# Twelve empty VectorE instructions ahead of the last two copies of a decode kernel

## The chip, the cores and the metric

One core of a Trainium2 chip (trn2). The metric is the device time of one execution in microseconds (us). A few executions of each kernel are compared on one chip.

## The reference, cut to what matters

One token goes through a pre-norm decoder block: attention over a cache of 32 heads x 4096 positions x 128, a residual, a layer norm, and a gated MLP with tanh GELU.

```python
x = A_x
h = x + _A_ref(_layernorm(x), A_k_cache, A_v_cache, A_wq, A_wo)
h2 = h + _B_ref(_layernorm(h), B_w_gate, B_w_up, B_w_down)   # GLU of 1728, down to 640
```

## The kernel before

The kernel records each operation with what it depends on, per engine, and emits waits and signals from that. Only its end matters here: the GLU product `hm`, the down projection, the copies and the store.

```python
ga = glu(ps_g, wg_sb, range(5), hl, d_wg)          # TensorE, 75 matmuls
glu(ps_u, wu_sb, range(3), d_wu[0])                # TensorE, 45
up = glu(ps_u, wu_sb, range(3, 5), d_wu[1])        # TensorE, 30
# ... GELU of the gate on VectorE and ScalarE, g1 to g8 ...
g6 = V(lambda e: e.tensor_mul(gu[:, :], g_t[:, :], t1[:, :]), g8)
g9 = V(lambda e: e.tensor_mul(hm[:, :], gu[:, :], ps_u[:, 0:15]), g6, up)
# ... down() : matmuls of hm with the down weights, 4 quarters of the result ...
T(down([13, 14]), g9, d_wp)
T(down(range(4)), d_wd[0])
T(down(range(4, 8)), d_wd[1])
T(down(range(8, 12)), d_wd[2])
dn = {q: T(down([12], [q]), d_wd[3]) for q in (0, 2, 1, 3)}
os = [V(lambda e, q=q: e.tensor_copy(out_row[0:1, 160 * q:160 * q + 160], ps_d[32 * q:32 * q + 1, 0:160]), dn[q])
      for q in range(2)]
os += [A(lambda e, q=q: e.copy(out_row[0:1, 160 * q:160 * q + 160], ps_d[32 * q:32 * q + 1, 0:160]), dn[q])
       for q in range(2, 4)]
d_out = P.dma("sync", out[0, :, :], out_row[:, :], *os)
```

`V`, `A`, `T` and `P.op` record an operation for VectorE, ScalarE, TensorE or a named engine; what follows the function are its dependencies.

The softmax here doesn't subtract the row's maximum and nothing guards it: scores larger than these inputs give would overflow.

Of the kernel before, what the change touches and what calls it, by code (L numbers as in the profile page):

```python
# [180 lines left out]
def bass_sequential_preLN__gqa_block_cached__glu_gated_geglu__decode_kernel(nc, A_x, A_k_cache, A_v_cache, A_wq, A_wo, B_x, B_w_gate, B_w_up, B_w_down, out):  # L181
# [60 lines left out]
    P = Prog(nc)  # L242
# [265 lines left out]
    g6 = V(lambda e: e.tensor_mul(gu[:, :], g_t[:, :], t1[:, :]), g8)  # L508
    g9 = V(lambda e: e.tensor_mul(hm[:, :], gu[:, :], ps_u[:, 0:15]), g6, up)

    def down(ms, qs=range(4)):
        def fn(e):
            for m in ms:
                for q in qs:
                    rows, wd = (128, wd_sb[:, m]) if m < 13 else (48, wd_lo[:, m - 13])
                    i = e.matmul(ps_d[32 * q:32 * q + 1, 0:160], hm[0:rows, m:m + 1],  # L516
                                 wd[0:rows, 160 * q:160 * q + 160], start=False, stop=(m == 12))
            return i
        return fn
# [5 lines that stand above are left out]
# [36 lines left out]
```

## Time and profile before

| | before |
|---|---|
| device time, 3 runs | 202.89 us median (202.81 to 203.33) |
| span of the profile | 201.4 us |
| last down weights landed | 198.64 us |
| VectorE idle between `hm` and its first copy | 3.12 us |
| TensorE idle for the last load | 0.61 us |

The first two rows are the whole, the last three are the place of the change. Here the loads set the end (transfers are 85% of the chain that ended last), so the engines have slack; the question is how much of it lies just where the change adds work. The profile lines for this are in the prediction.

### The profile page before, as it was taken

The page shows a single profiled execution, that of the slowest core. Times are in us where ns is not written, and L with a number is a line of the kernel's source. Part 1 is how long each engine was busy: PE and PEld are TensorE (multiplying, and loading weights), DVE is VectorE, ACT ScalarE, POOL GpSimd, SP SyncE. Part 2 cuts the span into 40 slices and gives each one's busy share as a digit, 9 for nine tenths or more (in the row PEclk, how much of TensorE's full clock was granted, in tenths as well). Part 3 has the DMA queues.
Part 4 walks back from the last instruction along what each step waited for, and adds up shares of the span by engine and source line. Part 5 has one row for each costly group of instructions (what it writes and reads, how often), then busy time and mean ns, then how long its engine had stood idle before and what let it go on. Part 6 is the DMA issues. An engine that isn't in the chain of part 4 may idle for free.

```text
span 201.4 us, 2003 instructions
## 1 busy us (share of the span) xinstructions
PE 119.7 (59%) x1009; PEld 33.8 (17%) x756; DVE 100.9 (50%) x51; ACT 12.6 (6%) x33; POOL 34.4 (17%) x36
## 2 busy tenths in 40 slices
PE   0107009659617943696299257907791697678684
PEld 0101000001200020112010201200201012268572
DVE  0200098983598079605970994199209933220321
ACT  2100000001000100010001001000000010010101
POOL 6400000000090018000900350053004400100000
PEclk9999757978966985589769859995599589685555
DMA  9989999999999999999999999999999999999992
GB/s 325 439 387 462 442 429 423 416 423 459 442 429 423 423 423 429 456 436 436 416 423 423 442 442 436 436 423 416 429 449 436 436 429 403 431 419 423 412 410 98
DMA packets 3848, 84.30 MB, mean 419 GB/s; under 512 B 450, under 2 KB 644, under 8 KB 1156
## 3 DMA queue, kind: packets, MB, share of 16 engines
q1 hardware_dynamic: 3842, 84.23, 97.8%
q8 instruction: 4, 0.07, 0.1%
q10 hardware_dynamic: 2, 0.00, 0.0%
HBM read 84.23 MB, written 0.00 MB: 418 GB/s over the span
## 4 chain that ended last, share of the span: by engine, by line
DMA 85%; PE 10%; SPq 4%; issue 0%; DVE 0%
DMA v_slot<-in_A_v_cache_dram 71%; DMA k_slot<-in_B_w_down_dram 13%; PE psum L363 9%; SPq L59 4%; PE psum L516 0%; DVE out_row L525 0%
## 5 line engine op out<-in xcount | busy, mean ns | idle before, releaser
L375 DVE TENSOR_TENSOR prod<-k_slot,qb 128x8192 bf16<-128x8192 bf16 x16 | 75.2, 4736 | 6.1 <-DMA k_slot<-in_A_k_cache_dram 6.1
L167 PE MATMUL psum<-prod,id_b 128*128 128x512 bf16 x233 | 65.0, 434 | 0.0
L381 DVE TENSOR_REDUCE sc<-psum 128x128 f32<-128x2048 f32 x8 | 18.3, 2291 | 50.7 <-PE psum L167 50.7
L385 POOL TENSOR_TENSOR p_bd<-pt,own 128x512 bf16<-128x512 bf16 x6 | 28.3, 4716 | 87.2 <-ACT pt L382 87.2
L352 PE MATMUL psum<-prod,id_b 128*128 128x512 bf16 x23 | 10.4, 452 | 49.4 <-DVE prod L375 46.2
L363 PE MATMUL psum<-v_slot,p_bd 128*16 128x512 bf16 x224 | 18.3, 484 | 7.4 <-DMA v_slot<-in_A_v_cache_dram 7.4
L352 PEld LDWEIGHTS psum<-prod,id_b 128*128 128x128 bf16 x23 | 2.3, 99 | 69.6 <-DVE prod L375 52.2
L369 PEld LDWEIGHTS psum<-hs,po_sb 128*128 128x128 f32 x64 | 8.3, 191 | 24.1 <-issue 23.5
L363 PEld LDWEIGHTS psum<-v_slot,p_bd 128*16 128x16 bf16 x224 | 5.8, 105 | 38.9 <-DMA v_slot<-in_A_v_cache_dram 30.7
L392 ACT COPY po_sb<-psum 128x512 f32<-128x512 f32 x7 | 4.1, 586 | 73.3 <-PE psum L363 73.3
L369 PE MATMUL psum<-hs,po_sb 128*128 128x4 f32 x64 | 7.7, 244 | 0.4 <-ACT po_sb L428 0.4
L382 ACT ACTIVATE pt<-sc,zero_t 128x128 bf16<-128x128 f32 x8 | 3.2, 401 | 70.4 <-DVE sc L381 70.4
L335 PE MATMUL psum<-arena,xlnB 128*32 128x512 bf16 x20 | 3.1, 579 | 7.3 <-DMA arena<-in_A_wq_dram 7.3
L465 PE MATMUL psum<-aP,arena 128*128 128x1 bf16 x160 | 6.7, 178 | 0.7 <-DMA arena<-in_A_wo_dram 0.6
L465 PEld LDWEIGHTS psum<-aP,arena 128*128 128x128 bf16 x160 | 6.6, 131 | 0.9 <-DMA arena<-in_A_wo_dram 0.7
L389 POOL MEMSET spare<- 1x1 f32 x1 | 0.1, 89 | 35.6 <-DVE p_bd L385 35.6
L494 PE MATMUL psum<-hlnT,v_slot 128*128 128x1 bf16 x150 | 5.5, 173 | 0.7 <-issue 0.7
L340 DVE CAST qb<-psum 128x512 bf16<-128x512 f32 x1 | 0.7, 692 | 9.8 <-PE psum L167 9.8
L494 PEld LDWEIGHTS psum<-hlnT,v_slot 128*128 128x128 bf16 x150 | 5.4, 120 | 1.3 <-issue 0.7
L363 PE MATMUL psum<-k_slot,p_bd 128*16 128x512 bf16 x32 | 3.5, 616 | 2.8 <-DVE p_bd L385 2.8
L308 PE MATMUL psum<-one_bf,x_row 1*128 1x1 bf16 x5 | 0.4, 177 | 7.1 <-DMA x_row<-in_A_x_dram 7.1
L311 DVE COPY xx<-psum 128x5 f32<-128x5 f32 x1 | 0.2, 165 | 7.5 <-PE psum L308 7.5
(73 smaller groups left out, 34.2 us busy)
## 6 DMA issues: line engine op xcount, KB each, us to landing
k_slot<-in_A_k_cache_dram SPq DMA_DIRECT2D x8, 4096.0 KB, 26.3
v_slot<-in_A_v_cache_dram SPq DMA_DIRECT2D x7, 4096.0 KB, 17.0
arena<-in_A_wq_dram SPq DMA_DIRECT2D x1, 5120.0 KB, 15.6
arena<-in_A_wo_dram SPq DMA_DIRECT2D x2, 2560.0 KB, 33.7
k_slot<-in_A_v_cache_dram SPq DMA_DIRECT2D x1, 4096.0 KB, 25.2
v_slot<-in_B_w_gate_dram SPq DMA_DIRECT2D x1, 2160.0 KB, 24.7
k_slot<-in_B_w_down_dram SPq DMA_DIRECT2D x3, 640.0 KB, 30.1
v_slot<-in_B_w_up_dram SPq DMA_DIRECT2D x1, 1296.0 KB, 27.4
```

What stands on the lines that cost most here:

```text
L59: ev = self.op(eng, lambda e: e.dma_start(out, in_), *deps, dma=True, chan=chan)
L167: built = e.matmul(out, lhsT, rhs, start=start, stop=stop)
L352: mm = held if n or not first else lambda e, *a, **k: e.matmul(*a, **k)
L363: i = e.matmul(ps_o[a:a + 16, :], p_bd[:, 4 * b:4 * b + 4, :].rearrange("p g j -> p (g j)"), vt[:, 4 * b:4 * b + 4, :], start=(b < 4), sto ...
L369: i = e.matmul(ps_a[:, bass.ds(at, 4)], po_sb[:, 128 * r:128 * r + 128], hs[:, r, :], start=(r == 0), stop=(r == 3))
L375: mults[G, i] = VM(lambda e: e.tensor_tensor(out=prod[:, i, :, :], in0=kt[:, 64 * i:64 * i + 64, :], in1=qb[:, G, :].unsqueeze(1).to_broad ...
L381: reds[G] = VR(lambda e: e.reduce_sum(sc[:, :], ps_f.rearrange("p (g d) -> p g d", d=16), axis=AX.X), folds[G, 1])
L382: exps[G] = AS(lambda e: e.activation(pt[:, :], sc[:, :], ACTF.Exp, bias=zero_t[:, 0:1], scale=INV_SQRT_DH, accum_out=RS[:, G:G + 1]), red ...
L385: blocks[G] = on(lambda e: e.tensor_tensor(out=p_bd[:, :, :], in0=pt[:, :].unsqueeze(2).to_broadcast([128, 128, 4]), in1=own[:, :].unsquee ...
L392: evs[G] = AS(lambda e: e.copy(po_sb[:, :], ps_o), pvs[G])
L465: r = e.matmul(ps_p[:, c:c + 1], wo_sb[:, i, c::5], aP[:, i:i + 1], start=False, stop=(i == 31), skip_group_check=True)
L494: i = e.matmul(ps[:, m:m + 1], ws, hlnT[:, c:c + 1], start=(c == 0 and m == 0), stop=(c == 4), skip_group_check=True)
```

## The change

The intent is to see what instructions that do nothing cost in VectorE's stream, at a place where VectorE has to wait. Each carries the flag `nofuse`.

```diff
     g9 = V(lambda e: e.tensor_mul(hm[:, :], gu[:, :], ps_u[:, 0:15]), g6, up)
 
+    def idle(eng, n):
+
+        def fn(e):
+            for _ in range(n):
+                i = e.nop(hint="n", nofuse=True)
+            return i
+        return P.op(eng, fn)
+    idle("vector", 12)
+
     def down(ms, qs=range(4)):
```

## The prediction

> **What bounds the kernel now.** I read the chain that ended last first, because an addition can cost only where it lengthens that chain, and took its shares from the page and its last pieces from the chain in order of time, cut to 163 to 201.5 us.
>
> ```profile
> span 201.4 us, 2003 instructions
> ...
> DMA 85%; PE 10%; SPq 4%; issue 0%; DVE 0%
> ```
>
> ```profile
> 171.63 27.02 DMA k_slot<-in_B_w_down_dram
> 198.64 0.04 issue
> 198.69 0.88 PE psum L516 x18
> 199.56 0.30 DVE out_row L525
> 199.86 0.03 issue
> 199.89 0.32 DVE out_row L525
> ```
>
> The transfers are 85% of the chain. The whole kernel is a stream of loads at a mean of 419 GB/s, and the last piece of the down weights lands at 198.64 us. What follows it is short and serial: the last down matmuls (0.88 us), two copies of the result on VectorE (0.30 and 0.32 us), then the store. VectorE is 50% busy over the span, but that average says nothing of this change: it adds VectorE work at one place only, so I read that place. It lies after the GLU product (L509, `hm`) and before the copies (L525). The timeline of VectorE alone, 196 to 201.4 us:
>
> ```profile
> 196.26 0.17 DVE L509 TENSOR_TENSOR hm<-gu,psum 128x15 bf16<-128x15 f32 x1 [1.86 <-PE psum L494]
> 199.55 0.66 DVE L525 CAST out_row<-psum 1x160 bf16<-1x160 f32 x2 [3.12 <-PE psum L516]
> ```
>
> The bracket is the number that decides the case: VectorE has nothing to do for 3.12 us (196.26 + 0.17 = 196.43 to 199.55), and what ends the idle time is TensorE's L516. What does TensorE do in that gap? The timeline of all engines, same stretch:
>
> ```profile
> 196.49 0.43 PE L516 MATMUL psum<-wd_lo,hm 48*1 48x160 bf16 x8 [0.33 <-DVE hm L509]
> ...
> 196.85 1.23 PE L516 MATMUL psum<-k_slot,hm 128*1 128x160 bf16 x32
> ...
> 198.69 0.83 PE L516 MATMUL psum<-k_slot,hm 128*1 128x160 bf16 x20 [0.61 <-DMA k_slot<-in_B_w_down_dram]
> ...
> 199.59 0.60 ACT L527 CAST out_row<-psum 1x160 bf16<-1x160 f32 x2 [5.89 <-PE psum L516]
> ```
>
> TensorE runs the down projection in three groups, and before the third it idles 0.61 us for the load that lands at 198.64 us. So the 3.12 us are held open at their far end by a DMA and 0.88 us of matmuls, neither of which asks VectorE for anything after `hm`. The other two quarters of the result are copied by ScalarE at 199.59 us and end at about the same time (199.59 + 0.60 = 200.19 against VectorE's 199.55 + 0.66 = 200.21).
>
> [...] No nop is in the trace of before[...]; its nearest relative there is the bare wait instruction on VectorE's sequencer:
>
> ```profile
> L114 DVEq EVENT_SEMAPHORE  x5: 21/21/116, 20.5 to 196.2; - x5
> ```
>
> Its columns are minimum, median and maximum in ns: 21 ns in the usual case. [...]
>
> **The change, part by part.** Removed: nothing. Moved: nothing; no load, buffer, semaphore or dependency changes. Added: 12 nops in VectorE's stream, which wait for nothing and signal nothing; they carry a flag[...], so I take all twelve to be there.
>
> Cost of the twelve, in three sizes, all estimates from numbers above:
> - Low: 12 x 21 ns = 0.25 us.
> - What I believe: [...]the pitch some two to three times the reported 21 ns, 40 to 65 ns, so 12 x 50 ns = 0.6 us. The factor is my choice; nothing in the trace gives it.
> - High: a nop that goes through VectorE's pipeline like a small dependent instruction. The timeline has such a row at 192.76, 192.97 and 193.18 us (L501, L502, L503, 128x15 each), a pitch of 0.21 us. 12 x 0.21 = 2.52 us.
>
> Where they lie: the first can start [...]when it has ended, 196.43 us. They are done by 196.43 + 0.6 = 197.03 us in the middle case and by 196.43 + 2.52 = 198.95 us in the high one. The first copy cannot start before 199.55 us. So 2.5 us of the gap stay unused in the middle case and 0.6 us in the high one. On the path: 0. `hm` stands before the nops in the same stream and signals when it ends, so TensorE gets it no later than now. Sum: 202.89 + 0 = 202.89 us.
>
> **The rivals.**
> 1. *The nops are dear.* The gap is used up at 3.12 / 12 = 260 ns each; beyond that every ns counts twelve times, as VectorE's copies end last. To reach 2% (0.02 x 202.89 = 4.06 us) each would have to take (3.12 + 4.06) / 12 = 598 ns. At 400 ns the time would be 202.89 + 4.8 - 3.12 = 204.6 us, still under 1% more. Against it: the 21 ns of a sequencer instruction, and that even a pass through the pipeline is 0.21 us.
> 2. *Code fetch.* Twelve more instructions could push VectorE's program over a block boundary and start a fetch late, among saturated queues. For it: the page shows fetches inside the span.
>
> ```profile
> q8 instruction: 4, 0.07, 0.1%
> ```
>
> Against it: [...]VectorE has 51 counted instructions[...]. And a fetch would come in a gap of 3 us. [...]
> 3. *`hm` is delayed.* If the twelve ran ahead of L509 or held its signal, the first two down groups would come later by 0.6 us, but TensorE idles 0.61 us for the last load anyway, so the time would stay at 202.9 us. For the high cost of 2.52 us it would be 202.89 + 2.52 - 0.61 = 204.8 us (+0.9%). Against it: program order, and the signal hangs on L509 itself.
> 4. *Faster.* Nothing is taken away, and the loads that carry the chain were all issued by 171.6 us, 25 us ahead of the nops. I see no way.
>
> **Range and chances.** The middle is the time of before, 202.9 us. The width is not from the nops but from the spread of runs: before has 202.81 to 203.33 us over three, 0.26%. I take that spread on both sides and a little more for another build and another day: 202.3 to 203.6 us. All rivals end inside 2% (206.95 us), so same gets 0.98, slower 0.01, faster 0.01.
>
> **What would show each step right or wrong.** Right: VectorE's idle time before its copies is still about 3.1 us and still ended by TensorE's L516 (some nine lines lower in the new numbering); the last load still lands about 27 us after its issue; the chain ends in load, matmuls, two copies; VectorE's count of busy instructions stays at 51 if nops are not counted as busy. The nops, if listed, should start near 196.3 us and be done before 197.5 us. Wrong: the first copy starts later than ScalarE's by more than 0.1 us, or its idle time is ended by something other than TensorE (then the nops are dear, rival 1); a fifth instruction block beside the gap (rival 2); TensorE's idle time before its last group gone and `hm` later against the landing of its inputs (rival 3). A change of the total by 0.3% with these unchanged would be a difference of the load stream, not of the nops.

The cost of the nops in the middle case, 12 x 50 ns = 0.6 us, stands as the estimate: 21 ns from the trace, times a factor that was chosen. "Pitch" is the time from one start to the next. "Saturated" is queue 1 at 97.8% on the page of before. What the trace after shows: the first nop started at 196.858 us, 0.03 us after `hm` started and while it ran (196.833 to 197.005 us), and TensorE's next matmul began 0.06 us after `hm` ended, before (196.43, 196.49 us) as after (197.00, 197.06 us).

## The result, and the profile after

The changed kernel took 202.76 us median (202.63 to 202.88, 4 runs), the kernel before 203.07 us (202.81 to 203.33, 4 runs); the ratio is 0.9984, 95% interval 0.9967 to 1.0002: the same. Ratios here are the mean time of one kernel's fast runs over that of the other's of the same rounds, so not quite the ratio of the medians quoted.

First the page of the changed kernel. The nine new lines of source move the down matmuls from L516 to L525 and the copies from L525 to L534, so one number names different things before and after.

```profile
span 201.5 us, 2014 instructions
...
PE 122.1 (61%) x1008; PEld 34.7 (17%) x756; DVE 100.9 (50%) x51; ACT 12.6 (6%) x33; POOL 34.4 (17%) x36
...
q8 instruction: 4, 0.07, 0.1%
q14 instruction: 1, 0.01, 0.0%
```

There are 2003 + 12 instructions, less one matmul record that this trace lacks (1008 for 1009). VectorE still counts 51: nops are not counted as busy. The last line is new; the experiments below tie it to VectorE's code. Next, all instructions of the nops' line, with minimum, median and maximum in ns, and first and last start:

```profile
L515 DVEq NOP  x12: 18/18/18, 196.9 to 197.8; - x12
```

All twelve are there, at 18 ns each, on VectorE's sequencer (`DVEq`). But 197.8 - 196.9 = 0.9 us is far more than 12 x 18 ns. The starts, read one by one from the trace's records, in us:

```
1 to 7:   196.858 196.905 196.951 196.998 197.045 197.092 197.139
8 to 12:  197.601 197.648 197.695 197.742 197.789
```

The pitch is 47 ns, and after the seventh the sequencer stands still for 0.44 us. Last, the timeline from `hm` on; the bracket is the idle time before a row and what ended it:

```profile
196.83 0.17 DVE L509 TENSOR_TENSOR hm<-gu,psum 128x15 bf16<-128x15 f32 x1 [2.00 <-PE psum L494]
...
197.42 2.19 PE L525 MATMUL psum<-k_slot,hm 128*1 128x160 bf16 x52
198.78 0.49 PEld L525 LDWEIGHTS psum<-k_slot,hm 128*1 128x1 bf16 x20 [0.47 <-DMA k_slot<-in_B_w_down_dram]
199.64 0.66 DVE L534 CAST out_row<-psum 1x160 bf16<-1x160 f32 x2 [2.64 <-PE psum L525]
199.68 0.60 ACT L536 CAST out_row<-psum 1x160 bf16<-1x160 f32 x2 [5.55 <-PE psum L525]
```

And the end of the chain that ended last, in order of time (start, length):

```profile
171.27 27.47 DMA k_slot<-in_B_w_down_dram
...
198.78 0.87 PE psum L525 x20
199.65 0.30 DVE out_row L534
...
199.99 0.32 DVE out_row L534
```

VectorE's idle time before the copies is still ended by TensorE and the chain still ends in load, matmuls and copies. The last nop ended at about 197.81 us, 1.8 us before the first copy. The gap is 2.64 us in place of 3.12 us because `hm` came 0.57 us later here; the nops cannot have done that, as the first of them started 0.03 us behind it (196.858 against 196.833 us), and in the repeat below, with the same twelve, `hm` came at 196.10 us. With `hm` so late one sign that the prediction gave for its rival 3 shows here: TensorE's matmuls have no idle time before their last 20, they stand in one row of 52, and only the weight loads (`PEld`) still wait 0.47 us for the load. In the repeat the matmuls wait 0.78 us, so this goes with the time at which `hm` comes, not with the nops.

### The profile page after: what moved, and what is told of

Read it like the earlier page. It is cut to its first block, busy times and chain, and to the rows that moved or that the text cites. A ratio compares the mean times of both kernels' runs of the same rounds, so it can differ in the third digit from the quotient of the medians.

```text
span 201.5 us, 2014 instructions
## 1 busy us (share of the span) xinstructions
PE 122.1 (61%) x1008; PEld 34.7 (17%) x756; DVE 100.9 (50%) x51; ACT 12.6 (6%) x33; POOL 34.4 (17%) x36
## 4 chain that ended last, share of the span: by engine, by line
DMA 68%; PE 19%; DVE 9%; SPq 3%; issue 1%; DVEq 0%
DMA v_slot<-in_A_v_cache_dram 42%; DMA k_slot<-in_B_w_down_dram 14%; DMA k_slot<-in_A_k_cache_dram 12%; PE psum L363 9%; PE psum L167 8%; DVE prod L375 6%; SPq L59 3%; DVE sc L381 2%; PE psum L352 1%; PE psum L525 0%; DVE out_row L534 0%; DVEq L114 0%
## 5 line engine op out<-in xcount | busy, mean ns | idle before, releaser
L167 PE MATMUL psum<-prod,id_b 128*128 128x512 bf16 x233 | 67.1, 445 | 0.0
L352 PE MATMUL psum<-prod,id_b 128*128 128x512 bf16 x23 | 10.6, 461 | 49.2 <-DVE prod L375 45.7
L363 PE MATMUL psum<-v_slot,p_bd 128*16 128x512 bf16 x224 | 17.8, 475 | 7.0 <-DMA v_slot<-in_A_v_cache_dram 7.0
L369 PEld LDWEIGHTS psum<-hs,po_sb 128*128 128x128 f32 x64 | 9.1, 208 | 23.9 <-issue 23.5
L369 PE MATMUL psum<-hs,po_sb 128*128 128x4 f32 x64 | 8.5, 256 | 0.1
L363 PE MATMUL psum<-k_slot,p_bd 128*16 128x512 bf16 x32 | 2.9, 520 | 2.8 <-DVE p_bd L385 2.8
```

The lines of the kernel that those rows point to most:

```text
L167: built = e.matmul(out, lhsT, rhs, start=start, stop=stop)
L352: mm = held if n or not first else lambda e, *a, **k: e.matmul(*a, **k)
L363: i = e.matmul(ps_o[a:a + 16, :], p_bd[:, 4 * b:4 * b + 4, :].rearrange("p g j -> p (g j)"), vt[:, 4 * b:4 * b + 4, :], start=(b < 4), sto ...
L369: i = e.matmul(ps_a[:, bass.ds(at, 4)], po_sb[:, 128 * r:128 * r + 128], hs[:, r, :], start=(r == 0), stop=(r == 3))
```

## The experiments

Two theories to begin with. Theory: the nops are free only because they lie in VectorE's gap. Rival: such instructions are free anywhere. And a second question that the profile after opened: is the 0.44 us, from here on "the stall", a boundary between blocks of VectorE's code, or something that comes with a run of nops?

**n12: the changed kernel again**, no edit, five rounds.

> The changed kernel again. Theory (the nops lie wholly in the gap of VectorE): ratio to before 1.000 within 0.003, the nops 12 x 18 ns with one stall of about 0.44 us after the seventh, VectorE still idle before its first copy and released by TensorE. Rival (the 0.16% of the first result were a real gain): ratio again 0.998 with an interval below 1.

Measured: 202.88 us (202.69 to 203.08), before 202.88 us; ratio 1.0003, interval 0.9989 to 1.0017. Again a stall of 0.444 us after the seventh nop. The 0.16% of the first result is noise.

**n3: three nops.**

```diff
-    idle("vector", 12)
+    idle("vector", 3)
```

> Three nops. Theory (the stall of 0.44 us after the seventh nop is a boundary between two blocks of VectorE's code, so it depends on the place in the stream): three nops at a pitch of 47 ns, 0.11 us from the first to the end of the last, no stall among them, no instruction packet on queue 14. Rival (the stall belongs to any run of nops, or was an accident of one execution): a stall also here, or none in n12. Time as before within 0.3%.

Measured: 202.83 us, ratio 0.9997. Three nops, no stall among them, no line for queue 14 on the page. As the theory had it. The trace's records do hold a packet on queue 14, but at 201.62 us, just after the span: with nine nops fewer, the place lies behind the copies.

**n100 and n200: a hundred and two hundred.**

```diff
-    idle("vector", 12)
+    idle("vector", 100)      # and 200
```

> A hundred nops. Theory (pitch 47 ns, one stall of 0.44 us, start 0.03 us after the start of the GLU product): the last nop ends at 0.03 + 99 x 0.047 + 0.44 + 0.02 = 5.1 us after that start; the first copy of before starts 3.29 us after it (199.55 - 196.26), the changed kernel's 2.81 us after it, so the copies and the end come 1.8 to 2.3 us later: 204.7 to 205.2 us, +0.9 to +1.2%, and VectorE's copies then end long after ScalarE's. Rival (the sequencer works nops off at no cost beside the gap, or drops them): time as before.

> Two hundred nops. Theory: another 100 x 47 ns = 4.7 us over n100, so +6.5 to +7.0 us over before, 209.4 to 210 us, +3.2 to +3.5%. If a block of code is 128 instructions[...], a second stall of 0.44 us comes after nop 135 (7 + 128), so 0.44 us more[...].

Measured: 204.41 us (ratio 1.0085, interval 1.0070 to 1.0101) and 209.71 us (ratio 1.0341, interval 1.0325 to 1.0357). The timeline of n100:

```profile
196.09 0.17 DVE L509 TENSOR_TENSOR hm<-gu,psum 128x15 bf16<-128x15 f32 x1 [1.66 <-PE psum L494]
...
199.61 0.60 ACT L536 CAST out_row<-psum 1x160 bf16<-1x160 f32 x2 [5.88 <-PE psum L525]
201.24 0.66 DVE L534 CAST out_row<-psum 1x160 bf16<-1x160 f32 x2 [4.97 <-issue]
```

ScalarE's copies start at 199.61 us as ever; VectorE's start 201.24 - 196.09 = 5.15 us after `hm` began, against 5.1 us expected. "issue" as releaser says that no other engine held it: the nops did. The time came 0.3 us under the range expected for it: in this execution `hm` was early and left 3.49 us to fill, so the copies moved by 5.15 - 3.49 = 1.66 us; measured were +1.53 us (for the difference see held12). From n200, two pieces of the chain that ended last, in order of time (start, length):

```profile
196.69 0.44 issue
...
203.10 0.40 issue
```

Two stalls; in the trace's records they are ahead of nop 8 and of nop 136, 128 instructions apart. Its page counts two packets on queue 14:

```profile
q14 instruction: 2, 0.02, 0.0%
```

So n200 has two stalls, 128 instructions apart, and one 8 KB packet of code for each: the stall belongs to a boundary in VectorE's code. The stall is not the wait for that packet, which in the records begins only 0.66 to 1.05 us after its stall has ended (nine stalls in eight profiles). What the sequencer waits for in the stall, no run here shows. From n100 to n200 the time grew by 5.30 us: 100 x 0.047 = 4.7, and the second stall of 0.40, makes 5.1 us; `hm` came 0.27 us later in the profile of n200 (196.37 against 196.09), which is about the rest.

**between: the twelve between the two copies.** The first copy is a VectorE instruction that waits for TensorE. Does the sequencer run nops behind it meanwhile?

```diff
-    idle("vector", 12)
-    os = [V(lambda e, q=q: e.tensor_copy(...), dn[q]) for q in range(2)]
+    os = []
+    for q in range(2):
+        os.append(V(lambda e, q=q: e.tensor_copy(...), dn[q]))
+        if q == 0:
+            idle("vector", 12)
```

> The twelve nops between the two copies. The first copy waits for TensorE until about 199.6 us. If VectorE's sequencer reads on past an instruction that stands waiting, the nops run at about 197 us, far before the first copy, and the end does not move: 203.0 us. If it stands still at the waiting copy, they run from about 199.6 us, last 11 x 0.047 + 0.44 + 0.02 = 1.0 us, and the second copy starts at about 200.65 us in place of 199.99 us: +0.65 us, +0.3%.

Measured: 203.40 us (203.29 to 203.54), before 202.93 us: +0.47 us for the +0.65 expected (the missing 0.2 us: see held12). Pieces of the chain around the boundary:

```profile
199.60 0.02 DVE out_row L535
199.62 0.04 issue
199.66 0.02 DVEq L515
...
199.85 0.02 DVEq L515
199.86 0.44 issue
200.31 0.02 DVEq L515
...
200.60 0.32 DVE out_row L535
```

The nops ran from 199.6 us, just after the first copy had started and while it still ran (it took 0.31 us), and the second copy came at 200.60 us. So here the nops behind the waiting copy waited with it (199.6 us and not 197), though not for its end (199.90 us). Six nops and the first copy make seven before the stall: once more the eighth instruction behind `hm`.

Eleven runs of before hold one of 204.88 us among ten of 202.77 to 203.01 us; it widens the intervals and pulls the ratios down by about 0.0009 ((204.88 - 202.9) / 11 = 0.18 us). For this and the next three kernels the medians are therefore the better measure; by their intervals alone the ratios are all unclear from 1 (between 1.0015, interval 0.9974 to 1.0055).

**held12: the twelve on the path.** The first waits for the matmul that the first copy waits for.

```diff
-    idle("vector", 12)
+    idle("vector", 12, dn[0])      # just ahead of os; idle() passes the dependency on
```

> The twelve nops again ahead of the copies, but the first waits for the same matmul as the first copy. Theory (nothing but the place made them free): they run on the path, from about 199.6 us, 12 x 0.047 = 0.56 us and the stall of 0.44 us: both copies and the end about 1.0 us later, 203.9 to 204.1 us, +0.5%; no VectorE idle time between nops and copies. Rival (such nops are free anywhere): +0.

Measured: 203.74 us (203.61 to 203.78), before 202.93 us: +0.81 us; ratio 1.0029, interval 0.9998 to 1.0059. From the chain that ended last, the stall and the first copy:

```profile
199.93 0.45 issue
...
200.63 0.31 DVE out_row L534
```

The nops began at 199.63 us and the first copy came at 200.63 us, 1.0 us later as expected. They are not free anywhere. The median rose by 0.2 us less than that. Most of it lies outside the span: device time less span (listed to 0.1 us for each run) is 1.26 us in the mean here against 1.40 us for the kernel before. It is 1.25 to 1.33 us in every kernel with nops on VectorE, and 1.40 to 1.47 us in the kernel before and pe20, which have none there. So times come out 0.1 to 0.3 us under what the shifts in the profiles give. What runs outside the span has no record, and the cause stays open.

**early_held: twelve free ones, then twelve held ones.**

```diff
     idle("vector", 12)
+    ...
+    idle("vector", 12, dn[0])      # just ahead of os
```

> Twelve free nops as in the change, then twelve that wait for the matmul. Theory (the stall belongs to the place in the stream): it now falls among the first, free twelve, and the held twelve cost only their pitch, 0.56 us: 203.5 to 203.6 us, 0.44 us less than the kernel with the held twelve alone although it has twelve nops more. Rival (the stall comes with any run of nops on the path): as slow as that kernel, or slower.

Measured: 203.34 us (203.30 to 203.41), ratio 1.0011, interval 0.9980 to 1.0041: 0.16 us under the range expected, and 0.40 us less than held12 with twelve nops more; the runs of the two do not overlap. From its chain, the first held nop and the first copy, with no piece over 0.04 us between them:

```profile
199.73 0.01 DVEq L515
...
200.30 0.31 DVE out_row L535
```
The stall fell ahead of nop 8, in the gap; from nop 13 at 199.72 us to the first copy at 200.30 us it took 0.58 us. The stall belongs to the place in the stream, and twelve nops more made the held ones cheaper by moving it.

**ahead_hm: the twelve in front of the GLU product.**

```diff
+    idle("vector", 12, g6, up)
     g9 = V(lambda e: e.tensor_mul(hm[:, :], gu[:, :], ps_u[:, 0:15]), g6, up)
-    idle("vector", 12)
```

> The twelve nops in front of the GLU product, the first of them waiting for what the product waits for, so that hm comes about 1.0 us later (12 x 0.047 + 0.44). TensorE's idle time for the last load was 0.61 us before and near 0.4 to 0.5 us in the changed kernel. Theory (that idle time takes up a late hm): the first two down groups shift, the idle time before the last group vanishes, and the end moves by only 0.4 to 0.6 us, +0.2 to +0.3%. Rival (hm is on the path): +1.0 us. Rival (all is hidden): +0.

Measured: 203.21 us (202.88 to 203.41), +0.28 us by the medians, ratio 1.0000, interval 0.9968 to 1.0031. From its timeline:

```profile
197.76 0.17 DVE L517 TENSOR_TENSOR hm<-gu,psum 128x15 bf16<-128x15 f32 x1 [2.90 <-issue]
...
198.35 1.56 PEld L525 LDWEIGHTS psum<-k_slot,hm 128*1 128x1 bf16 x52 [0.26 <-issue]
198.35 1.90 PE L525 MATMUL psum<-k_slot,hm 128*1 128x160 bf16 x52
```

The nops held `hm` for 1.0 us (first nop 196.77, product 197.76). Now the weight loads too, and not only the matmuls as in the changed kernel, are one group of 52 with no wait for the load: the slack has been used up. From `hm` to the first copy it took 2.52 us, against 3.29 us before, so the slack before was 0.77 us, a little more than the 0.61 us for which the matmuls idle; by the same difference it was 0.29 us in the profile after and 0.94 us in n12. The stall fell ahead of the ninth nop, and not the eighth, as it must if it belongs to a place in the stream: the product no longer stands ahead of them.

The interval does not part the theory from the rival that all is hidden; the direct evidence is that group. The six runs fall into two sets, 202.88 to 203.05 us and 203.36 to 203.41 us, and the profile is of the run of 203.41 us: there it was +0.48 us, as expected, in the other set -0.05 to +0.12 us. My estimate from the slacks is 0.99 less 0.29 to 0.94, so 0.05 to 0.7 us; that the slack parts the two sets is not shown, as one run alone was kept as a profile.

**n6: half as many as the change.**

```diff
-    idle("vector", 12)
+    idle("vector", 6)
```

> Six nops, half as many as the change. The runs so far put the stall of 0.44 us before the eighth instruction behind hm, and showed that the nops between the copies ran only once the first copy had started. Theory (both hold): seventh is the first copy and eighth the second; the sequencer meets the boundary only after it has let the first copy go at 199.6 us, so the stall stands on the path: the second copy starts about 0.025 + 0.045 + 0.44 = 0.5 us after the first in place of 0.34 us, and the end comes 0.15 to 0.2 us later than with twelve nops (+0.1%, to be read from the profile). No idle time of 0.44 us among the nops. Rival (the sequencer crosses the boundary ahead of time, or the stall needs nops around it): 0.34 us between the copies as ever.

Measured: 202.82 us (202.74 to 202.89), ratio 0.9994, interval 0.9980 to 1.0007. The theory fell: 0.34 us between the two copies as ever, no stall between them:

```profile
199.61 0.30 DVE out_row L534
...
199.95 0.32 DVE out_row L534
```

The packet of code that followed each stall so far gives an estimate of when the boundary was crossed. The transfers of n6, cut to 196 to 199.5 us, so ahead of its first copy at 199.60 us:

```profile
q14 instruction: 1, 0.01, 0.5%
```

In "between" that packet is not in this stretch but after 199.6 us. In the changed kernel it began 0.69 us after the stall's end (198.29 against 197.60), in n6 at 198.19 us. With the 0.66 to 1.05 us seen elsewhere the boundary was crossed by about 197.5 us in n6 (an estimate, 198.19 - 0.66), just behind the last nop (197.01) and 2 us before the first copy. So, by the packet's time, as reading itself leaves no record, the sequencer had read on to the second copy while the first stood waiting. By that estimate the waiting copy of n6 did not keep the sequencer from reading the next copy; in "between" it kept the nops from running until 199.6 us. How far ahead it reads, no run here shows.

**pe20: twenty nops on TensorE ahead of the GLU matmuls**, none on VectorE.

```diff
+    idle("tensor", 20)
     ga = glu(ps_g, wg_sb, range(5), hl, d_wg)
...
-    idle("vector", 12)
```

> No nops on VectorE, twenty on TensorE ahead of the GLU matmuls. In every profile so far TensorE has an idle time of 0.4 to 0.85 us without a releaser ahead of the last 6 of the 150 GLU matmuls. Theory (it is the same kind of code boundary, there at a fixed place of TensorE's stream): twenty instructions more move it by ten pairs of weight load and matmul, to ahead of the last 16. Rival (it is tied to the data, such as the landing of the up weights): it stays ahead of the last 6, or near there in time. The end as before within 0.3% either way, as the last load sets it.

Measured: 203.86 us (203.54 to 204.18), ratio 1.0047, interval 1.0028 to 1.0066. The timeline of before, then that of pe20:

```profile
195.78 0.37 PE L494 MATMUL psum<-hlnT,v_slot 128*128 128x1 bf16 x6 [0.67 <-issue]
```

```profile
197.14 0.69 PE L494 MATMUL psum<-hlnT,v_slot 128*128 128x1 bf16 x16 [1.36 <-issue]
197.94 0.17 DVE L517 TENSOR_TENSOR hm<-gu,psum 128x15 bf16<-128x15 f32 x1 [2.54 <-PE psum L494]
```

The idle time moved from ahead of the last 6 to ahead of the last 16, by ten pairs: so here it went with the place in TensorE's stream too. That half held. The half about the end did not. I had let the last load take it all up, but the twenty nops (first and last start 189.4 and 190.8 us) delayed the start of the GLU matmuls (190.99 against 189.97 us) and the stall grew from 0.67 to 1.36 us, so `hm` came 1.68 us later than in the profile before. Less the slack of 0.77 us (from `hm` to the first copy it took 2.52 us, as in ahead_hm) that is 0.91 us, by which the copies came later; the median rose by 0.99 us. Why the stall is longer there stays open.

## Why the prediction was right

The time was right, 202.76 us in 202.3 to 203.6, and so was the mechanism. Step by step:

- *What bounds the end.* The last load, 0.88 us of matmuls and the copies, with VectorE's gap held open from outside: so in the profile after. n100 and n200 show that the gap ends where it was said to: past it each nop counts (5.30 us for the second hundred, a stall of 0.40 us among them).
- *The cost of twelve.* The pitch was put at 40 to 65 ns, by a factor of choice over 21 ns; it is 47 ns, so 12 x 0.047 = 0.56 us for the 0.6 us of the middle case. That the factor was right is luck, and nothing hung on it: any pitch under 260 ns fits the gap. The 21 ns is a duration, and a duration said little of the pitch: the nops last 18 ns each and start 47 ns apart. And the twelve took 0.95 us, because of the stall, which was not in that sum. The finish "before 197.5 us" was missed in the first profile (197.81 us) for that, and because `hm` came later; in n12 they ran from 196.12 to 197.07 us.
- *On the path: 0.* Shown by n12 and n3, with an interval of about 0.15% either way.
- *Rival 1, dear nops.* Refuted by the 47 ns. Held on the path the twelve cost 0.8 us by the medians and 1.0 us in the profile, 0.4 to 0.5%, so place and not cheapness makes them free.
- *Rival 2, code fetch.* The argument against it was wrong: VectorE's few counted instructions, 51, were held against a boundary, and a boundary did come, at the eighth instruction behind `hm`, with a stall of 0.44 us. What saved the number was the other half of the argument, that it would fall in a gap of 3 us. On the path it would have cost 0.4 us, by held12 against early_held.
- *Rival 3, a late `hm`.* The nops did not delay it. The slack ahead of the last load is real (ahead_hm, pe20), but the 0.61 us read off the matmuls was not a fixed amount: that idle time was 0.78 us in n12, 0.16 us in n6 and gone in the first profile after.

## What to carry to other kernels

Ask of added work first whether it lies in a gap and what ends that gap: twelve nops added nothing measurable behind the product and about 0.8 us one wait later in the same stream. Count the instructions of an engine's stream too, not only its work: here a boundary in VectorE's code stalled its sequencer for 0.40 to 0.45 us, and twelve nops more in the stream decided that this fell in the gap and not on the path (early_held 203.34 us, held12 203.74 us).
